# A long convolution with gate and MLP: filter steps three groups apart, and ten pieces of the second batch ahead of the first MLP block

## The chip, the cores and the metric

One NeuronCore of a Trainium2 chip runs the whole program. The metric is the device time of one execution in microseconds. A core has a matrix engine (TensorE, PE in the rows), a vector engine (VectorE, DVE), an activation engine (ScalarE, ACT), a general engine (GpSimd, POOL) and a queue for transfers (SyncE, SP). Each takes its instructions in the order in which the program issues them; between engines there are semaphores.

## The reference

```
h_filt = (relu(pos_emb @ w1) @ w2) * exp(-0.01 * pos)       # (12480, 128)
u = x * v                                                   # (4, 12480, 128)
y = irfft(rfft(u, 2S) * rfft(h_filt, 2S))[:, :S]            # a causal convolution of length S = 12480
a = (x * y).reshape(49920, 128)
h = a @ w_in                                                # (49920, 2048)
g = where(h > 0, h, exp(min(h, 0)) - 1)
out = g @ w_out                                             # (49920, 128)
```

x, v and pos_emb are float32; w_in and w_out are float64, and the kernel converts them itself from pairs of 32-bit words.

## The kernel before, in words

The sequence is seen as 2 x 104 x 60 (w, N1, N2). The convolution is a transform along N1 (a matrix product with a 104 x 104 table, three products of split float32 each, `mm3`), a transform along N2 with a table for every k, a product with the spectrum of the filter, and the two inverses. Between the two directions data goes through DRAM (`a_d`, `h_d`, `f_d`, `b_d`), which turns it.

The program has three parts, each issued in an order written out by hand.

1. **First part**, `stage1` with `first` set, batch 0. 15 groups of input (`g`), each with four pieces (i: two results r, two halves w of the sequence). One piece is one `mm3` into a PSUM tile `aps` and a copy to `a_sb`; `store` sends `a_sb` to `a_d`. Two pieces together are a turn, `q = 2 * g + r`, and every turn also does one of the 30 groups of the filter (class `Filter`): `step` 0 transposes `pos` into `pt` and copies it (ScalarE, `pt_sb`), `step` 1 multiplies by w1 into `rp` and applies Relu (ScalarE, `r_sb`), `step` 2 multiplies by w2 into `hps`, applies the window (VectorE, `h_sb`) and splits into `h_h` (ScalarE) and `h_l` (VectorE). `transform` multiplies by the table into `Hps` (two PSUM banks), which leaves as `hsb` (ScalarE, then VectorE) to `h_d`. In the turns 0 to 15 `weights` converts a piece of w_in or w_out on VectorE (lines 303 to 313) and `split_w` splits the one before (a copy on ScalarE, a subtraction on POOL, line 324). `gate` forms x * v (line 102; POOL from the third group on), `split` its two parts `u_h` (ScalarE) and `u_l` (VectorE, line 111).
2. **Second part**, `stage2` with `first` set: the N2 transforms of batch 0, the filter's spectrum, the product, the inverse, to `b_d`.
3. **MLP**, `Mlp.run`: 120 blocks of 416 tokens with 8 steps each; one step is an `up_proj` (`fps`), `elu`, `split_lo`, `down_proj` (`ops`). `conv_out` does the last inverse of a block (`yps`), `transp` turns it. Beside the steps run side generators: `side[0]` to `side[2]` do `stage1` and `stage2` for the batches 1 to 3, at 1.08 pieces a step, each within the 240 steps of the batch before it.

What sets the order in the first part is the loop of lines 143 to 183 and, ahead of it, lines 121 to 140. In before a turn issues for the next filter group q+1:

```
filt.step(q + 1, 2 * w)       # line 154: step 0 in the first piece, step 2 in the second
...
filt.step(q + 1, 1)           # line 166: step 1, after the first piece
```

Of the kernel before, what the change touches and what calls it, by code (L numbers as in the profile page):

```python
# [14 lines left out]
D = 128  # L15
# [23 lines left out]
def fftconv_gate_elu_mlp_kernel(ctx: ExitStack, tc: tile.TileContext, x, v, pos_emb, w1, w2,  # L39
# [41 lines left out]
    def stage1(st, h, ps_pool, ps_tag, first):  # L81
        Z = 1 if first else 2
        xv = st.enter_context(tc.tile_pool(name=f"xv{h}", bufs=3 if first else 2))
        up = st.enter_context(tc.tile_pool(name=f"up{h}", bufs=2))
        ap = st.enter_context(tc.tile_pool(name=f"ap{h}", bufs=4 if first else 3))
        ld, us, stores = {}, {}, []

        def load(g):
            if g >= NG:
                return  # L90
            xt = xv.tile([N1, 2, G, D], F32, tag="xt", name="xt")
            vt = xv.tile([N1, 2, G, D], F32, tag="vt", name="vt")
            nc.sync.dma_start(out=xt, in_=xq[:, :, h, g * G:(g + 1) * G, :])
            nc.sync.dma_start(out=vt, in_=vq[:, :, h, g * G:(g + 1) * G, :])
            ld[g] = (xt, vt)

        def gate(g):
            if g >= NG:
                return
            xt, vt = ld[g]  # L100
            e = nc.vector if first and g < 2 else nc.gpsimd
            e.tensor_tensor(out=vt, in0=xt, in1=vt, op=ALU.mult)

        def split(g):
            if g >= NG:
                return
            vt = ld.pop(g)[1]
            u_h = up.tile([N1, 2, G, D], F32R, tag="u_h", name="u_h")
            u_l = up.tile([N1, 2, G, D], F32R, tag="u_l", name="u_l")
            copy(u_h, vt)  # L110
            nc.vector.tensor_tensor(out=u_l, in0=vt, in1=u_h, op=ALU.subtract)
            us[g] = (u_h, u_l)

        def store():
            if stores:
                g, r, t = stores.pop()
                nc.sync.dma_start(out=a_d[h][:, r, g * G:(g + 1) * G].rearrange("k n z c -> k (n z c)"),
                                  in_=t.bitcast(F32).rearrange("k n z w d -> k (n z w d)"))

        if first:  # L120
            filt = Filter(st)
            for g in range(4):
                filt.load(g)
                if g < 3:
                    load(g)
                filt.load_w(g)
            gate(0)
            gate(1)
            for q in range(3):
                filt.step(0, q)  # L130
        else:
            load(0)
            load(1)
            for _ in range(4):
                yield
            gate(0)
            gate(1)
            yield
            yield
        split(0)  # L140
        if not first:
            yield
        for g in range(NG):
            if first:
                gate(g + 2)
            u_h, u_l = us.pop(g)
            for i in range(4):
                r, w = divmod(i, 2)
                f = FWD[w][r]
                if w == 0:  # L150
                    a_sb = ap.tile([N1, G, Z, 2, D], F32 if first else F32R, tag="a_sb", name="a_sb")
                if first:
                    q = 2 * g + r
                    filt.step(q + 1, 2 * w)
                ps = ps_pool.tile([N1, 512], F32, tag=ps_tag, name="aps")
                mm3(ps, dft_h[:, f, :], dft_l[:, f, :], u_h[:, w], u_l[:, w])
                src = ps.rearrange("p (n d) -> p n d", n=G)
                if first and w == 0:
                    nc.vector.tensor_copy(out=a_sb[:, :, 0, w], in_=src)
                else:  # L160
                    copy(a_sb[:, :, 0, w], src)
                if not first:
                    nc.vector.tensor_tensor(out=a_sb[:, :, 1, w], in0=src, in1=a_sb[:, :, 0, w], op=ALU.subtract)
                if first:
                    if w == 0:
                        filt.step(q + 1, 1)
                        filt.load(q + 4)
                        filt.load_w(q + 4)
                    else:
                        filt.transform(q)  # L170
                        filt.weights(q)
                        filt.split_w(q - 1)
                if w == 0:
                    store()
                else:
                    stores.append((g, r, a_sb))
                if i == 0:
                    load(g + (3 if first else 2))
                if i == 1:
                    split(g + 1)  # L180
                if i == 2 and not first:
                    gate(g + 2)
                yield
        store()
        if first:
            filt.flush()


    class Filter:
# [2 lines left out]

        def __init__(self, st):
            c1 = st.enter_context(tc.tile_pool(name="c1", bufs=1))
            self.pp = st.enter_context(tc.tile_pool(name="pp", bufs=5))
            self.hp = st.enter_context(tc.tile_pool(name="hp", bufs=1))
            self.wl = st.enter_context(tc.tile_pool(name="wl", bufs=1))
            self.psh = st.enter_context(tc.tile_pool(name="psh", bufs=2, space=PS))
            self.psH = st.enter_context(tc.tile_pool(name="psH", bufs=1, space=PS))
            self.w1 = c1.tile([64, 64], F32, name="w1_sb")  # L200
            self.w2 = c1.tile([64, D], F32, name="w2_sb")
            self.win = c1.tile([N1, 2, N2], F32, name="win_sb")
            nc.scalar.dma_start(out=self.w1, in_=w1)
            nc.scalar.dma_start(out=self.w2, in_=w2)
            nc.scalar.dma_start(out=self.win, in_=window)
            self.pos, self.t, self.hs, self.zs, self.out = {}, {}, {}, {}, []
# [8 lines left out]
        def step(self, g, q):  # L215
# [2 lines left out]
            hp, psh = self.hp, self.psh  # L218
            if q == 0:
                p = self.pos.pop(g)  # L220
                pt = psh.tile([64, 2 * GF, N1], F32, tag="h", name="pt")
                for n in range(2 * GF):
                    nc.tensor.transpose(out=pt[:, n, :], in_=p[:, n // GF, n % GF, :], identity=id_sb[:N1, :N1])
                pt_sb = hp.tile([64, 2 * GF, N1], F32, tag="pt_sb", name="pt_sb")
                copy(pt_sb, pt)
                self.t[g] = pt_sb
            elif q == 1:
                rp = psh.tile([64, 2 * GF, N1], F32, tag="h", name="rp")
                nc.tensor.matmul(out=rp, lhsT=self.w1, rhs=self.t[g], start=True, stop=True)
                r_sb = hp.tile([64, 2 * GF, N1], F32, tag="r_sb", name="r_sb")  # L230
                nc.scalar.activation(out=r_sb, in_=rp, func=ACTF.Relu)
                self.t[g] = r_sb
            elif q == 2:
                r_sb = self.t.pop(g)
                hps = psh.tile([N1, 2, GF, D], F32, tag="h", name="hps")
                for n in range(2 * GF):
                    nc.tensor.matmul(out=hps[:, n // GF, n % GF, :], lhsT=r_sb[:, n, :], rhs=self.w2,
                                     start=True, stop=True)
                h_sb = hp.tile([N1, 2, GF, D], F32, tag="h_sb", name="h_sb")
                nc.vector.tensor_tensor(  # L240
                    out=h_sb, in0=hps,
                    in1=self.win[:, :, g * GF:(g + 1) * GF].rearrange("p w (n o) -> p w n o", o=1).to_broadcast([N1, 2, GF, D]),
                    op=ALU.mult)
                h_h = hp.tile([N1, 2, GF * D], F32R, tag="h_h", name="h_h", bufs=2)
                h_l = hp.tile([N1, 2, GF * D], F32R, tag="h_l", name="h_l", bufs=2)
                hv = h_sb.rearrange("p w n d -> p w (n d)")
                copy(h_h, hv)
                nc.vector.tensor_tensor(out=h_l, in0=hv, in1=h_h, op=ALU.subtract)
                self.hs[g] = (h_h, h_l)

        def transform(self, g):
# [21 lines left out]
        def load_w(self, i):  # L273
# [1 line left out]
            if i >= self.NW:  # L275
                return
            m, c = divmod(i, DFF // WC)
            z = self.wl.tile([128, WC, 2], U32, tag="z", name="z", bufs=5)
            if m == 0:
                src = w_in[:, c * WC:(c + 1) * WC].bitcast(U32)  # L280
                nc.sync.dma_start(out=z.rearrange("p f t -> p (f t)"), in_=src)
# [199 lines left out]
    class Mlp:  # L481
# [12 lines left out]
        def run(self, side, alone):  # L494
# [111 lines left out]
                    b, w, n = blocks[j]  # L606
                    nc.sync.dma_start(out=oq[:, w, b, n * G:(n + 1) * G, :], in_=o)

            for i in range(2):
                load(i)  # L610
            split_b(0)
            split_b(1)
            conv_out(0)
# [54 lines left out]
    with ExitStack() as st:  # L668
# [3 lines left out]
        nc.scalar.dma_start(out=id_sb, in_=ident)  # L672
        copy(dft_h, dft_sb)
        nc.vector.tensor_tensor(out=dft_l, in0=dft_sb, in1=dft_h, op=ALU.subtract)
        psa = st.enter_context(tc.tile_pool(name="psa", bufs=4, space=PS))
        for _ in stage1(st, 0, psa, "a", True):
            pass
    with ExitStack() as st:
# [68 lines left out]
```

## Time and profile before

| | |
|---|---|
| median of 3 runs | 3584.68 us (3576.38 to 3588.11) |
| profiled execution | 3582.95 us, span 3581.2 us |
| busy over the span | PE 3411.3 us (95%), DVE 3156.0 (88%), ACT 2416.0 (67%), POOL 2280.5 (64%) |
| mean granted TensorE clock | 0.975 of 2.4 GHz |
| DMA | 646.30 MB, mean 180 GB/s |

The span runs from the first to the last instruction. Busy shares are means over three parts with different limits, so they are read part by part below. In the rows a time in square brackets is the idle time of the engine just before the instruction, with what ended it; `x4` counts instructions in one row; matmuls overlap, so their own times add up to more than the distance between their starts.

### The profile page before, as it was taken

How to read it: one execution, taken by the hardware profiler on the slowest of the kernel's cores; microseconds unless marked ns; L12 is line 12 of the kernel's file. 1: busy time of each engine (PE TensorE's matmuls, PEld its weight loads, DVE VectorE, ACT ScalarE, POOL GpSimd, SP SyncE). 2: the span in 40 equal slices, each digit the busy share in tenths (PEclk: the TensorE clock that was granted, in tenths of full speed). 3: DMA queues.
4: the chain of work that ended last, by engine and by line, in shares of the span. 5: the costliest groups of instructions: out<-in, count | busy, mean ns of one | idle time of the engine just before them, and what ended most of it. 6: DMA issues, size and time to landing. Idle time of an engine off the chain costs nothing.

```text
span 3581.2 us, 53363 instructions
## 1 busy us (share of the span) xinstructions
PE 3411.3 (95%) x18444; PEld 3153.7 (88%) x18444; DVE 3156.0 (88%) x3941; ACT 2416.0 (67%) x3290; POOL 2280.5 (64%) x1578
## 2 busy tenths in 40 slices
PE   7887888999999999999999999999999999999999
PEld 5666777889899899889999998889999999999998
DVE  5647988999999999999999989989999988888887
ACT  3334546877666677876666677776666677777776
POOL 3406876667777766557677656567676656666565
PEclk7789998999999999999999999999999999999999
DMA  6558876767787744777788746778888842222221
GB/s 185 172 146 245 267 243 175 225 181 210 201 223 215 203 131 143 248 228 216 225 245 230 227 127 175 250 206 227 231 241 225 232 116 58 68 62 58 72 58 27
DMA packets 383995, 646.30 MB, mean 180 GB/s; under 512 B 24678, under 2 KB 170438, under 8 KB 374366
## 3 DMA queue, kind: packets, MB, share of 16 engines
q1 hardware_dynamic: 383305, 642.73, 63.3%
q8 instruction: 147, 2.41, 0.3%
q14 instruction: 122, 1.00, 0.1%
q10 hardware_dynamic: 421, 0.16, 0.0%
HBM read 412.76 MB, written 230.03 MB: 179 GB/s over the span
## 4 chain that ended last, share of the span: by engine, by line
PE 60%; DVE 9%; DMA 7%; issue 4%; ACT 1%; POOL 1%; SPq 1%; POOLq 0%; DVEq 0%; ACTq 0%
PE fps L53 8%; PE fps L55 8%; PE fps L54 8%; PE ops L53 7%; PE ops L54 7%; PE ops L55 7%; DMA al<-a_d 4%; PE bps L445 3%; DVE g_l L576 3%; DVE g L567 2%; PE xps L53 2%; PE xps L55 2%; PE xps L54 2%; DMA vt<-in_v_dram 2%; PE yps L53 1%
## 5 line engine op out<-in xcount | busy, mean ns | idle before, releaser
L570 POOL CAST g_h<-g 128x832 fp32r<-128x832 f32 x960 | 1225.0, 1280 | 979.3 <-DVE g L567 978.7
L560 ACT ACTIVATE n<-fps 128x832 f32<-128x832 f32 x960 | 832.0, 867 | 742.1 <-PE fps L55 723.6
L567 DVE SCALAR_TENSOR_TENSOR g<-n,fps 128x832 f32<-128x832 f32 x960 | 975.2, 1016 | 224.1 <-ACT n L561 219.9
L576 DVE TENSOR_TENSOR g_l<-g,g_h 128x832 fp32r<-128x832 f32 x960 | 1111.2, 1157 | 19.6 <-POOL g_h L570 19.6
L561 ACT ACTIVATE n<-n 128x832 f32<-128x832 f32 x960 | 864.5, 901 | 30.5
L53 PE MATMUL fps<-t_h,wi_h 128*128 128x416 f32 x1920 | 715.6, 373 | 22.4 <-DVE g L567 21.2
L53 PE MATMUL ops<-g_h,wo_h 128*128 128x416 f32 x1920 | 677.0, 353 | 0.5 <-ACT o_sb L58 0.3
L55 PE MATMUL fps<-t_h,wi_l 128*128 128x416 f32 x1920 | 676.0, 352 | 0.0
L54 PE MATMUL fps<-t_l,wi_h 128*128 128x416 f32 x1920 | 675.6, 352 | 0.0
L54 PE MATMUL ops<-g_l,wo_h 128*128 128x416 f32 x1920 | 674.8, 351 | 0.7 <-DVE g_l L576 0.7
L55 PE MATMUL ops<-g_h,wo_l 128*128 128x416 f32 x1920 | 675.1, 352 | 0.0
L426 POOL TENSOR_TENSOR p<-p 120x768 f32<-120x768 f32 x204 | 483.3, 2369 | 76.6 <-DVE p L420 57.7
L53 PEld LDWEIGHTS fps<-t_h,wi_h 128*128 128x128 f32 x1920 | 362.8, 189 | 56.9 <-DVE g L567 36.7
L54 PEld LDWEIGHTS fps<-t_l,wi_h 128*128 128x128 f32 x1920 | 364.6, 190 | 13.4 <-DVE t_l L549 0.3
L53 PEld LDWEIGHTS ops<-g_h,wo_h 128*128 128x128 f32 x1920 | 361.7, 188 | 6.0 <-POOL g_h L570 0.8
L54 PEld LDWEIGHTS ops<-g_l,wo_h 128*128 128x128 f32 x1920 | 362.2, 189 | 4.3 <-DVE g_l L576 1.4
L55 PEld LDWEIGHTS fps<-t_h,wi_l 128*128 128x128 f32 x1920 | 362.1, 189 | 3.1
L55 PEld LDWEIGHTS ops<-g_h,wo_l 128*128 128x128 f32 x1920 | 360.8, 188 | 4.0
L418 DVE TENSOR_TENSOR p<-xps,f 120x512 f32<-120x512 f32 x416 | 283.4, 681 | 10.5 <-ACT a_h L58 4.1
L427 POOL TENSOR_TENSOR p<-p 120x256 f32<-120x256 f32 x204 | 249.4, 1222 | 16.0
L445 PE MATMUL bps<-p,t 120*120 120x256 f32 x832 | 219.5, 386 | 30.5 <-POOL p L427 26.1
L353 DVE TENSOR_TENSOR tl<-t,th 120x360 fp32r<-120x360 f32 x208 | 214.5, 1032 | 25.6 <-ACT th L58 25.4
(95 smaller groups left out, 4966.1 us busy)
## 6 DMA issues: line engine op xcount, KB each, us to landing
a_d<-a_sb SPq DMA_DIRECT2D x90, 832.0 KB
al<-a_d SPq DMA_DIRECT2D x156, 480.0 KB
f<-f_d SPq DMA_DIRECT2D x312, 240.0 KB
b_d<-b_sb SPq DMA_DIRECT2D x156, 480.0 KB
b<-b_d SPq DMA_DIRECT2D x90, 832.0 KB
t<-in_tab_dram SPq DMA_DIRECT2D x208, 281.2 KB
xt<-in_x_dram SPq DMA_DIRECT2D x60, 416.0 KB
vt<-in_v_dram SPq DMA_DIRECT2D x60, 416.0 KB
```

What stands on the lines that cost most here:

```text
L53: nc.tensor.matmul(out=ps, lhsT=hi, rhs=bh, start=start, stop=False)
L54: nc.tensor.matmul(out=ps, lhsT=hi, rhs=bl, start=False, stop=False)
L55: nc.tensor.matmul(out=ps, lhsT=lo, rhs=bh, start=False, stop=stop)
L418: nc.vector.tensor_tensor(out=p[:, :, :2], in0=ps[:, :, 0:1, :].to_broadcast([RI, TG, 2, D]), in1=f[:, :, r], op=ALU.mult)
L426: e.tensor_tensor(out=q, in0=q, in1=p, op=ALU.add)
L427: e.tensor_tensor(out=q[:, :, 1], in0=q[:, :, 1], in1=q[:, :, 2], op=ALU.add)
L445: nc.tensor.matmul(out=ps[:, o], lhsT=t[:, o, 3 * N2:], rhs=y[:, o, :2], start=True, stop=True)
L560: nc.scalar.activation(out=n, in_=ps[:, :, :NT], func=ACTF.Relu, scale=-1.0)
L561: nc.scalar.activation(out=n, in_=n, func=ACTF.Exp, scale=-1.0)
L567: nc.vector.scalar_tensor_tensor(out=g, in0=n, scalar=-1.0, in1=ps[:, :, :NT], op0=ALU.add, op1=ALU.max)
L570: nc.gpsimd.tensor_copy(out=g_h, in_=g)
L576: nc.vector.tensor_tensor(out=g_l, in0=g, in1=g_h, op=ALU.subtract)
```

## The change

```diff
@@ stage1: split
-            nc.vector.tensor_tensor(out=u_l, in0=vt, in1=u_h, op=ALU.subtract)
+            e = nc.gpsimd if first and g else nc.vector
+            e.tensor_tensor(out=u_l, in0=vt, in1=u_h, op=ALU.subtract)
@@ stage1: ahead of the loop
-            for g in range(4):
+            for g in range(5):
                 filt.load(g)
...
             gate(0)
+            for q in range(3):
+                for i in range(3 - q):
+                    filt.step(i, q)
             gate(1)
-            for q in range(3):
-                filt.step(0, q)
         else:
             load(0)
             load(1)
-            for _ in range(4):
+            for _ in range(4 if h > 1 else 0):
                 yield
             gate(0)
             gate(1)
-            yield
-            yield
+            for _ in range(2 if h > 1 else 0):
+                yield
@@ stage1: the loop
-                    filt.step(q + 1, 2 * w)
+                    filt.step(q + 3 - w, w)
...
                     if w == 0:
-                        filt.step(q + 1, 1)
-                        filt.load(q + 4)
-                        filt.load_w(q + 4)
+                        filt.step(q + 1, 2)
+                        filt.load(q + 5)
                     else:
                         filt.transform(q)
-                        filt.weights(q)
-                        filt.split_w(q - 1)
+                        if q % 2 == 0 or q == 1:
+                            c = (q + 1) // 2 + (q > 1)
+                            filt.load_w(c + 5)
+                            filt.weights(c)
+                            filt.split_w(c - 1)
...
         if first:
+            filt.split_w(filt.NW - 1)
             filt.flush()
@@ Filter
-            self.pp = st.enter_context(tc.tile_pool(name="pp", bufs=5))
+            self.pp = st.enter_context(tc.tile_pool(name="pp", bufs=6))
-            self.psh = st.enter_context(tc.tile_pool(name="psh", bufs=2, space=PS))
+            self.psh = st.enter_context(tc.tile_pool(name="psh", bufs=1, space=PS))
-                pt = psh.tile([64, 2 * GF, N1], F32, tag="h", name="pt")
+                pt = psh.tile([64, 2 * GF, N1], F32, tag="t", name="pt")
-                rp = psh.tile([64, 2 * GF, N1], F32, tag="h", name="rp")
+                rp = psh.tile([64, 2 * GF, N1], F32, tag="r", name="rp")
...
-                nc.vector.tensor_tensor(out=h_l, in0=hv, in1=h_h, op=ALU.subtract)
+                nc.gpsimd.tensor_tensor(out=h_l, in0=hv, in1=h_h, op=ALU.subtract)
...
-            z = self.wl.tile([128, WC, 2], U32, tag="z", name="z", bufs=5)
+            z = self.wl.tile([128, WC, 2], U32, tag="z", name="z", bufs=6)
@@ Mlp.run
-            for i in range(2):
-                load(i)
+            for _ in range(1):
+                next(side[0])
+            load(0)
+            load(1)
+            for _ in range(9):
+                next(side[0])
             split_b(0)
             split_b(1)
             conv_out(0)
@@ the first part's PSUM pool
-        psa = st.enter_context(tc.tile_pool(name="psa", bufs=4, space=PS))
+        psa = st.enter_context(tc.tile_pool(name="psa", bufs=3, space=PS))
```

`pt_sb`, `r_sb` and `h_sb` get two buffers each (one before). In PSUM `pt`, `rp` and `hps` have a bank each, where they shared a ring of two, and the transforms' tiles are three, where they were four. A turn now issues `step` 0 of group q+3, `step` 2 of group q+1 and `step` 1 of group q+2. The conversion of the weights stands in turns 0, 1, 2, 4, 6, ... 28, no longer in turns 0 to 15. `u_l` (from the second group on) and `h_l` go from VectorE to POOL. The first ten `next(side[0])` are: the loads, gates and split of the first two groups of batch 1, then nine pieces (27 matmuls).

TensorE in a turn of the first part's loop: the transposes, the first piece's `mm3`, then what stands between it and the second piece's.

```order
-L223 MATMUL pt<-id_sb,pos 64x104 x4
-L53 MATMUL aps<-u_h,dft_h 104x512
-L54 MATMUL aps<-u_l,dft_h 104x512
-L55 MATMUL aps<-u_h,dft_l 104x512
-L229 MATMUL rp<-pt_sb,w_sb 64x416
-L237 MATMUL hps<-w_sb,r_sb 104x128 x4
+L228 MATMUL pt<-id_sb,pos 64x104 x4
+L53 MATMUL aps<-u_h,dft_h 104x512
+L54 MATMUL aps<-u_l,dft_h 104x512
+L55 MATMUL aps<-u_h,dft_l 104x512
+L242 MATMUL hps<-w_sb,r_sb 104x128 x4
+L234 MATMUL rp<-pt_sb,w_sb 64x416
```

`hps` has moved ahead of `rp`, and the two belong to different groups: the `r_sb` that `hps` reads is from the turn before, and so is the `pt_sb` that `rp` reads.

POOL in the loop, two pairs of turns of before:

```order
L324 TENSOR_TENSOR wi_l<-r,wi_h 128x256 x2
L102 TENSOR_TENSOR vt<-xt,vt 104x1024
L324 TENSOR_TENSOR wi_l<-r,wi_h 128x256 x2
L102 TENSOR_TENSOR vt<-xt,vt 104x1024
L324 TENSOR_TENSOR wi_l<-r,wi_h 128x256
```

and the same two pairs with the change:

```order
L112 TENSOR_TENSOR u_l<-vt,u_h 104x1024
L253 TENSOR_TENSOR h_l<-h_sb,h_h 104x512
L102 TENSOR_TENSOR vt<-xt,vt 104x1024
L253 TENSOR_TENSOR h_l<-h_sb,h_h 104x512
L329 TENSOR_TENSOR wi_l<-r,wi_h 128x256
L112 TENSOR_TENSOR u_l<-vt,u_h 104x1024
L253 TENSOR_TENSOR h_l<-h_sb,h_h 104x512
L102 TENSOR_TENSOR vt<-xt,vt 104x1024
L253 TENSOR_TENSOR h_l<-h_sb,h_h 104x512
```

A pair had one gate (L102) and two subtractions of the weights; it has one gate, one subtraction of the weights, one `u_l` and two `h_l`, with `u_l` right behind the weights.

SP from the second part's last stores on, before (`b_d` to `b` and `x` are the blocks of the MLP, `xt` and `vt` batch 1):

```order
L435 DMA b_d_61<-b_sb 120x2x256 x2
L513 DMA b_5089<-b_d_61 104x8x128
L514 DMA x_5088<-in_x_dram 104x512
L513 DMA b_5094<-b_d_61 104x8x128
L514 DMA x_5093<-in_x_dram 104x512
L513 DMA b_5121<-b_d_61 104x8x128
L514 DMA x_5120<-in_x_dram 104x512
L93 DMA xt<-in_x_dram 104x2x512
L94 DMA vt<-in_v_dram 104x2x512
```

and with the change:

```order
L440 DMA b_d_61<-b_sb 120x2x256 x2
L93 DMA xt<-in_x_dram 104x2x512
L94 DMA vt<-in_v_dram 104x2x512
L93 DMA xt<-in_x_dram 104x2x512
L94 DMA vt<-in_v_dram 104x2x512
L518 DMA b_5112<-b_d_61 104x8x128
L519 DMA x_5111<-in_x_dram 104x512
L518 DMA b_5117<-b_d_61 104x8x128
L519 DMA x_5116<-in_x_dram 104x512
L93 DMA xt<-in_x_dram 104x2x512
L94 DMA vt<-in_v_dram 104x2x512
```

Batch 1's first two groups are now asked for ahead of the MLP's first two blocks, and its third ahead of the MLP's third block. On TensorE the nine pieces stand between the second part's last `bps` and the first `yps`.

## Rows read from the trace of the kernel before

**Rows 1.** Stretches: bounds, length, busy PE, PEld, DVE, ACT, POOL; clock, DMA share, GB/s.

```profile
21.00:268.00 247.00, 213.29 (x938) 158.75 (x938) 143.55 (x291) 96.18 (x175) 78.46 (x29) 0.76 0.56 165
320.00:340.00 20.00, 17.99 (x102) 15.41 (x101) 18.46 (x26) 11.14 (x22) 15.84 (x18) 1.00 0.89 279
553.00:567.00 14.00, 11.47 (x58) 9.87 (x57) 12.03 (x11) 10.07 (x13) 10.46 (x7) 1.00 0.41 95
```

**Rows 2.** One line's instructions: line 159, shortest/median/longest ns, first and last start.

```profile
L159 DVE COPY a_sb<-aps x30: 676/679/692, 21.3 to 266.7; 104x512 f32<-104x512 f32 x30
```

**Rows 3.** Order of time on TensorE, first part: start us, length us, instruction.

```profile
228.55 0.91 PE L229 MATMUL rp<-pt_sb,w_sb 64*64 64x416 f32 x2
230.06 1.12 PE L237 MATMUL hps<-w_sb,r_sb 64*104 64x128 f32 x8 [0.60 <-ACT r_sb L231]
...
233.31 0.52 PE L223 MATMUL pt<-id_sb,pos 104*64 104x104 f32 x4
233.60 0.46 PE L53 MATMUL aps<-u_h,dft_h 104*104 104x512 f32 x1
...
235.50 0.91 PE L229 MATMUL rp<-pt_sb,w_sb 64*64 64x416 f32 x2 [0.98 <-ACT pt_sb L58]
...
238.07 0.75 PE L53 MATMUL aps<-u_h,dft_h 104*104 104x512 f32 x1
```

**Rows 4.** Waits, 21 to 268 us: total us, times, longest.

```profile
PE hps L237 <- ACT r_sb L231: 17.4, 29, 0.6
PE rp L229 <- ACT pt_sb L58: 16.2, 18, 1.5
```

**Rows 5.** Stretches of the MLP, lines 163 (first row) and 567 alone: DVE busy (count).

```profile
600.00:650.00 50.00, 10.26 (x16) 1.00 0.77 240
...
600.00:650.00 50.00, 14.15 (x14) 1.00 0.77 240
3050.00:3100.00 50.00, 20.39 (x20) 1.00 0.26 66
```

**Rows 6.** Order of time on TensorE, the MLP's first steps.

```profile
557.16 0.45 PE L53 MATMUL fps<-t_h,wi_h 128*128 128x416 f32 x1 [1.39 <-DVE g L567]
...
571.22 0.48 PE L54 MATMUL aps<-u_l,dft_h 104*104 104x512 f32 x1 [2.62 <-DVE u_l L111]
```

**Rows 7.** Order of time on POOL, first part.

```profile
163.88 3.00 POOL L324 TENSOR_TENSOR wo_l<-r,wo_h 128x256 fp32r<-128x256 f32 x1 [6.97 <-ACT wo_h L58]
...
170.38 0.72 POOL L324 TENSOR_TENSOR wo_l<-r,wo_h 128x256 fp32r<-128x256 f32 x1 [0.95 <-ACT wo_h L58]
171.06 2.34 POOL L102 TENSOR_TENSOR vt<-xt,vt 104x1024 f32<-104x1024 f32 x1
```

**Rows 8.** Order of time on POOL, the MLP's first steps.

```profile
560.62 2.40 POOL L524 TENSOR_TENSOR b<-b,b 104x1024 fp32r<-104x1024 f32 x1
...
564.60 5.48 POOL L102 TENSOR_TENSOR vt<-xt,vt 104x1024 f32<-104x1024 f32 x2
...
582.12 3.43 POOL L102 TENSOR_TENSOR vt<-xt,vt 104x1024 f32<-104x1024 f32 x1
```

**Rows 9.** Groups by line and form, 40 to 268 us: busy us, mean ns.

```profile
L58 ACT ACTIVATE hsb<-Hps 104x512 f32<-104x512 f32 x27 | 16.1, 596 | 37.9 <-PE Hps L55 37.9
...
L58 ACT ACTIVATE wi_h<-r 128x256 fp32r<-128x256 f32 x8 | 3.3, 410 | 0.0
```

**Rows 10.** Order of time on all engines, the start.

```profile
9.89 0.31 SPq L212 DMA_DIRECT2D pos<-in_pos_emb_dram  x1
...
15.37 1.23 DVE L102 TENSOR_TENSOR vt<-xt,vt 104x1024 f32<-104x1024 f32 x1 [4.84 <-DMA vt<-in_v_dram]
```

**Rows 11.** Order of time on all engines, from the second part to the MLP.

```profile
530.42 3.63 SPq L435 DMA_DIRECT2D b_d<-b_sb  x2
...
541.14 1.06 ACT L58 ACTIVATE b<-b 104x1024 fp32r<-104x1024 f32 x1 [7.43 <-DMA b<-b_d]
...
548.60 0.72 PE L53 MATMUL fps<-t_h,wi_h 128*128 128x416 f32 x1 [0.65 <-ACT t_h L58]
```

More of the change, by code (lines that the diff above doesn't have):

```diff
@@ L220, in step @@
                 p = self.pos.pop(g)
-                pt = psh.tile([64, 2 * GF, N1], F32, tag="h", name="pt")
+                pt = psh.tile([64, 2 * GF, N1], F32, tag="t", name="pt")
                 for n in range(2 * GF):
                     nc.tensor.transpose(out=pt[:, n, :], in_=p[:, n // GF, n % GF, :], identity=id_sb[:N1, :N1])
-                pt_sb = hp.tile([64, 2 * GF, N1], F32, tag="pt_sb", name="pt_sb")
+                pt_sb = hp.tile([64, 2 * GF, N1], F32, tag="pt_sb", name="pt_sb", bufs=2)
                 copy(pt_sb, pt)
@@ L227, in step @@
             elif q == 1:
-                rp = psh.tile([64, 2 * GF, N1], F32, tag="h", name="rp")
+                rp = psh.tile([64, 2 * GF, N1], F32, tag="r", name="rp")
                 nc.tensor.matmul(out=rp, lhsT=self.w1, rhs=self.t[g], start=True, stop=True)
-                r_sb = hp.tile([64, 2 * GF, N1], F32, tag="r_sb", name="r_sb")
+                r_sb = hp.tile([64, 2 * GF, N1], F32, tag="r_sb", name="r_sb", bufs=2)
                 nc.scalar.activation(out=r_sb, in_=rp, func=ACTF.Relu)
@@ L238, in step @@
                                      start=True, stop=True)
-                h_sb = hp.tile([N1, 2, GF, D], F32, tag="h_sb", name="h_sb")
+                h_sb = hp.tile([N1, 2, GF, D], F32, tag="h_sb", name="h_sb", bufs=2)
                 nc.vector.tensor_tensor(
```

## The prediction

> **What bounds the kernel now.** I read the stretches of the span first, then the order of time on TensorE inside the first part, then the waits, then the other engines at the two places that the change touches. A *turn* is one filter group with its two transform pieces (lines 147 to 183); there are 30 turns, and two of them, a *pair*, use one group of input.
>
> The first part runs to 268 us. It keeps TensorE busy 213 of 247 us, but at a mean granted clock of 0.76, and moves only 165 GB/s; the second part holds 1.00 and 279 GB/s [rows 1]. So in the first part neither the DMA nor one engine is full. The column copies on line 159 give the pace: 30 of them from 21.3 to 266.7 us, (266.7 - 21.3)/29 = 8.46 us a turn [rows 2]. At full clock one turn shows its make-up: from the `rp` at 228.55 to the `rp` at 235.50 are 6.95 us, in which TensorE waited 0.60 for `r_sb` and 0.98 for `pt_sb` [rows 3]. Its own work is thus 6.95 - 0.60 - 0.98 = 5.37 us. Each wait is a ScalarE copy between two products of the same filter group that stand one behind the other in TensorE's queue; 29 and 18 such waits are in this stretch [rows 4]. After such a turn, at 238.07, a matmul of the same transform takes 0.75 us in place of 0.46 at 233.60 [rows 3]: the waits are paid a second time, through the clock, which goes to 1.2 GHz.
>
> The MLP that follows is bound by TensorE and VectorE together. While side pieces run, 14 MLP steps fit in 50 us and 16 pieces beside them; alone, 20 steps fit [rows 5]. So 50/14 - 50/20 = 1.07 us a step is the price of 16/14 = 1.14 pieces: 0.94 us a piece.
>
> **The change, first part.** The filter's three products of one turn now belong to groups q+3, q+1 and q+2 and have a PSUM bank each, so that every ScalarE copy has most of a turn to finish. Both waits of 0.60 and 0.98 go, and what is late next has to be found.
>
> TensorE: unchanged work, 5.37 us a turn, if the clock stays up. It should: between 553 and 567 us there was a single wait of 1.39 us [rows 6], and the clock of that stretch is 1.00 [rows 1].
>
> POOL takes over `h_l` (each turn) and `u_l` (each pair). The product of 1024 columns takes POOL 2.34 and the subtraction of 256 takes 0.72, which a straight line puts at 1.26 for the 512 columns of `h_l`; bounds 0.72 and 2.34 [rows 7]. `u_l` has the form of POOL's subtraction on line 524, 2.40 [rows 8]. The subtraction of the weights takes 3.00 in 15 of 16 cases, and 0.72 the one time that VectorE converts no weights beside it [rows 7]; in the new order it starts beside a conversion as before, so I take 3.00. In a pair: 3.00 + 2.40 + 2.34 + 2 x 1.26 = 10.3 us, where it had 8.3 at most. VectorE loses `u_l` and two `h_l` a pair and is not waited for.
>
> What is late next is `u_l`. After the last `Hps` of a pair's first turn come ScalarE's `hsb` 0.60, the copy of the weights 0.41 [rows 9], POOL 3.00 for the weights and 2.40 for `u_l`, sum 6.4; I add 0.3 because ScalarE comes to `hsb` late (its `h_h` stands behind VectorE's conversion), 6.7. TensorE meanwhile does a turn, 5.37, and in the next one `pt`, 0.29 from its start to the next, and the first of three matmuls, 0.46 with its tail and some 0.3 without [rows 3], 5.96, and then waits 0.75. A pair is 2 x 5.37 + 0.75 = 11.5 us, POOL's 10.3 fits in it, and a turn is 5.75; I take 5.8. Bounds: 5.37 (no wait) and 6.2 (POOL's `h_l` at 2.34, 12.4 a pair).
>
> DMA: 247 us at 165 GB/s are 40.8 MB, 1.40 MB a turn, which at 5.8 us is 241 GB/s, under the 279 seen [rows 1]. Loads of x and v are asked for about a pair ahead, 11.6 us.
>
> On moving such work to POOL, row and rule part in what they advise. The same product takes VectorE 1.23 [rows 10] and POOL 2.34 [rows 7]. The Trainium skill, "GPSIMD Engine Reference", section "Engine selection", says that elementwise work with two inputs belongs on VectorE, since POOL is about twice as slow. Followed, it would save the 0.75 us of waiting in each of 14 pairs, 11 us; by the rows the sum still falls by the 69 us below, because VectorE's queue is freed of it.
>
> The sum: 29 x (8.46 - 5.8) = 77 us gained. Against it: the first three turns all carry a conversion, one more than the pattern, 3 us (one subtraction at 3.00; bounds 0 and 6). And the start: three groups are transposed first, and the third `pos` was issued at 9.89, behind the second v, which landed at 15.37 [rows 10]. Before, the first group was through its products by then. Now two `rp` and one `hps` come behind, 2 x 0.91 + 1.12 = 2.9 us at full clock, 5.9 at half [rows 3]; I take 5. First part: -77 + 3 + 5 = **-69 us**.
>
> **The change, the ten pieces.** Before, the last store of the second part was issued at 534.05 (530.42 + 3.63), the first block's b was copied at 541.14, and `fps` began at 548.60, 7.5 later [rows 11]. Now four loads of x and v go ahead of b on SP, and 27 matmuls ahead of `conv_out(0)` on TensorE. The ninth computing piece needs the third x and v, whose buffer is free only after the first `u_l`. Of the 7.1 us from the last store to b's copy I give the load 5 (an estimate: the store had to land first). So loads from 534.05 land at 539, then product 2.34, copy about 1, `u_l` 1.23: 543.7. Its load goes behind b; at 5 to 8 us (an estimate from the same 7.1) it lands at 549 to 552, and product, copy, `u_l` and one transform (5.3) put the ninth piece at 554 to 557. Then 7.5 to the first `fps`: 563.5, **15 later** (bounds 10 and 18). In return nine pieces leave the MLP, 9 x 0.94 = 8.5, and so do the two gates that held POOL 5.48 us at 564.60 [rows 8]; TensorE waited 2.62 for the `u_l` behind them [rows 6]. I credit 4, that and some of the other waits of the start-up (bounds 0 and 6). Sum +15 - 8.5 - 4 = +2.5, bounds -4.5 and +9.5. What hides the pieces is the time in which TensorE waited for b; if the loads land late, the delay is bare.
>
> **Sum.** -69 + 2.5 = -66.5. The profiled execution took 3582.95 us (span 3581.2), so 3516.5; the median of the runs shown is 1.7 higher, so **3518 us**.
>
> **Rivals.**
> 1. *The clock stays low.* Speaks for it: three PSUM tiles for the transforms in place of four, one bank per product, and a wait of 0.75 in each pair. Against: the wait of 1.39 us at a clock of 1.00, above [rows 1, 6]. If 0.76 stays, a turn is 5.37/0.76 = 7.1 us, 29 x 1.3 = 38 more: **3556**. The Trainium skill, "TensorE: Matmul & The Clock Gate", section "A second HAM failure mode: psum-queue depth-cycling", describes short idle gaps between groups of matmuls that make the clock swing; by that rule this case would come, while the trace shows it only where two waits stand in one turn. Chance 0.12.
> 2. *POOL never holds TensorE.* The weights' subtraction slips past the conversion (0.72) and a turn is 5.37: 29 x 0.43 = 12 less, **3506**. Chance 0.15.
> 3. *POOL becomes the bound, and slower than before.* Every POOL instruction of a pair is stretched as the weights' subtraction is (by 3.00 - 0.72 = 2.28 for each `h_l`, so 3.5) and as a gate at 582.12 (3.43) [rows 8]: 3.00 + 2 x 3.43 + 2 x 3.5 = 16.9 us, and with 1.2 us for the copies that it waits for a pair is 18.1, a turn 9.0: 29 x 3.2 = 93 more, **3611**. It decides from 16.9 us a pair, the present pace. The Trainium skill, "SBUF — State Buffer", section "Who interferes with whom", has VectorE and POOL lock each other out of a shared port; the trace agrees for the weights' subtraction, 3.00 against 0.72 [rows 7]. Against it: conversions fill only 16 of 30 turns, and a gate without one beside it ran at 2.34 [rows 7]. Chance 0.04.
> 4. *The first part is the DMA's.* If its pattern gives no more than 165 GB/s, the pace stays and only start and pieces count: 3584.7 + 8 + 2.5 = **3595**. Against: the share of 0.56 [rows 1]. Chance 0.04.
>
> **How the numbers follow.** The forecast has 0.65; its own range is 3502 to 3540 (5.4 to 6.2 us a turn, the pieces between -4.5 and +9.5). The range takes in rivals 1 and 2: 3498 to 3558, leaving out the last two and some tails. A measurement of this kernel tells about 0.3%, 11 us, from no change: faster 0.65 + 0.12 + 0.15 = 0.92, the same 0.04 (rival 4), slower 0.04 (rival 3).
>
> **What would show it.** Right: line 161's copies 5.6 to 6.1 us apart, a clock over 0.9 and over 220 GB/s in the first part, the waits of `rp` and `hps` for ScalarE gone, a wait of TensorE for POOL's `u_l` once a pair, the second part beginning about 70 us sooner and lasting the same; from the second part's last store to the first `fps` some 29 us in place of 14.6, and the second batch's transforms done nine pieces sooner. Wrong: a clock near 0.76 without those waits (rival 1), POOL over 0.9 busy (rival 3), DMA share near 0.9 with TensorE idle (rival 4), or an MLP that begins late and gains nothing back.

## The result and the profile after

The changed kernel takes 3550.92 us (median of 5 runs, 3544.8 to 3554.95), against 3580.65 us for the kernel before in the same comparison: a ratio of 0.9916, 95% interval 0.9895 to 0.9937. That is 30 us faster, where 67 us were forecast. The time lies within the stated range of 3498 to 3558 us.

The stretches of the changed kernel (bounds, length, busy PE, PEld, DVE, ACT, POOL; clock, DMA share, GB/s): first the loop of the first part, then a piece of it, then one of the places where the clock falls.

```profile
29.00:228.00 199.00, 186.15 (x931) 132.64 (x929) 105.82 (x247) 89.88 (x172) 147.46 (x71) 0.87 0.66 201
29.00:57.00 28.00, 27.61 (x120) 19.48 (x119) 15.40 (x38) 10.13 (x19) 17.17 (x8) 1.00 0.59 164
...
101.00:114.00 13.00, 13.00 (x44) 9.45 (x44) 5.32 (x14) 5.50 (x10) 9.93 (x6) 0.50 0.66 221
```

The loop's clock is 0.87, where it was 0.76 [rows 1], and it is a mixture: 1.00 in most places, 0.50 in five stretches of 7 to 14 us, which add up to 51 us. In those TensorE is busy without a gap. The first turns are a sixth such stretch that the column does not show. It says 1.00 from 29 us on, but up to 46 us the matmuls have the lengths that they have at 0.50, and a turn, from one `pt` to the next, takes 9.57 us (order of time on TensorE):

```profile
36.91 0.90 PE L228 MATMUL pt<-id_sb,pos 104*64 104x104 f32 x4
37.49 0.73 PE L53 MATMUL aps<-u_h,dft_h 104*104 104x512 f32 x1
...
46.48 0.52 PE L228 MATMUL pt<-id_sb,pos 104*64 104x104 f32 x4
46.78 0.46 PE L53 MATMUL aps<-u_h,dft_h 104*104 104x512 f32 x1
```

The first turns of the other kernels are like this too (up to 30 us in before, up to 38.5 in e9 below), so a clock given here for a loop leaves them out.

The copies that give the pace, by their line (shortest/median/longest ns, first and last start), answering to [rows 2]:

```profile
L161 DVE COPY a_sb<-aps x30: 676/680/692, 29.5 to 228.1; 104x512 f32<-104x512 f32 x30
```

(228.1 - 29.5)/29 = 6.85 us a turn, where 8.46 stood and 5.8 was forecast. The first copy is 8.2 us later than before.

TensorE's waits in the loop (total us, times, longest), answering to [rows 4]:

```profile
PE aps L54 <- POOL u_l L112: 9.0, 10, 2.0
PE hps L242 <- ACT r_sb L236: 2.7, 2, 2.3
```

The waits for ScalarE's copies are gone but for two; a wait for POOL's `u_l` has come. The longer of the two for `r_sb`, 2.29 us at 140.74, has an origin like those of e3 below: an instruction of VectorE's conversion beside POOL's `u_l` took 2.61 us (135.35), and `h_sb`, `h_h` and `r_sb` came late behind it. How a wait for `u_l` goes is to be seen in the order of time on TensorE:

```profile
87.15 0.47 PE L54 MATMUL aps<-u_l,dft_h 104*104 104x512 f32 x1 [0.85 <-POOL u_l L112]
...
98.67 0.48 PE L54 MATMUL aps<-u_l,dft_h 104*104 104x512 f32 x1 [0.85 <-POOL u_l L112]
...
105.27 0.90 PE L228 MATMUL pt<-id_sb,pos 104*64 104x104 f32 x4
107.37 2.03 PE L242 MATMUL hps<-w_sb,r_sb 64*104 64x128 f32 x8
...
114.80 0.52 PE L228 MATMUL pt<-id_sb,pos 104*64 104x104 f32 x4
115.95 1.12 PE L242 MATMUL hps<-w_sb,r_sb 64*104 64x128 f32 x8
...
120.01 0.52 PE L228 MATMUL pt<-id_sb,pos 104*64 104x104 f32 x4
```

Two waits of 0.85 us, one pair apart. After the first the clock stays up; after the second it falls, and the turn from 105.27 to 114.80 takes 9.5 us, with no wait in it. The turn from 114.80 to 120.01, at full clock again, takes 5.2.

POOL, in the same pair, does what the prediction had it do (start, length):

```profile
93.08 3.02 POOL L329 TENSOR_TENSOR wi_l<-r,wi_h 128x256 fp32r<-128x256 f32 x1 [1.04 <-ACT wi_h L58]
96.06 2.56 POOL L112 TENSOR_TENSOR u_l<-vt,u_h 104x1024 fp32r<-104x1024 f32 x1
98.58 1.27 POOL L253 TENSOR_TENSOR h_l<-h_sb,h_h 104x512 fp32r<-104x512 f32 x1
99.81 2.36 POOL L102 TENSOR_TENSOR vt<-xt,vt 104x1024 f32<-104x1024 f32 x1
```

At the other place, from the second part to the MLP, the order of time on all engines, answering to [rows 11]:

```profile
495.18 0.32 SPq L440 DMA_DIRECT2D b_d<-b_sb  x1
...
502.29 2.34 POOL L102 TENSOR_TENSOR vt<-xt,vt 104x1024 f32<-104x1024 f32 x1 [12.01 <-DMA vt<-in_v_dram]
505.77 0.76 PE L53 MATMUL aps<-u_h,dft_h 104*104 104x512 f32 x1 [11.30 <-ACT u_h L58]
507.00 0.32 SPq L94 DMA_DIRECT2D vt<-in_v_dram  x1
515.21 2.38 POOL L102 TENSOR_TENSOR vt<-xt,vt 104x1024 f32<-104x1024 f32 x1 [6.00 <-DMA vt<-in_v_dram]
520.59 0.75 PE L53 MATMUL aps<-u_h,dft_h 104*104 104x512 f32 x1 [1.70 <-DVE a_sb L165]
529.89 0.71 PE L53 MATMUL fps<-t_h,wi_h 128*128 128x416 f32 x1 [0.61 <-ACT t_h L58]
```

From the end of the last store's issue (495.5) to the first `fps` are 34.4 us, 19.8 more than before. The MLP from its first to its last `fps` (line 53, first and last start), before and after:

```profile
L53 PE MATMUL fps<-t_h,wi_h x1920: 346/353/716, 548.6 to 3568.5; 128*128 128x416 f32 x192
```

```profile
L53 PE MATMUL fps<-t_h,wi_h x1920: 346/353/713, 529.9 to 3538.6; 128*128 128x416 f32 x192
```

3019.9 and 3008.7 us: 11.2 regained. So the profiled execution, 29.9 us shorter, splits into +8.2 (start), -46.8 (29 turns), about 0 (from the loop to the second part's end) and +8.6 (pieces: 19.8 - 11.2). Forecast: +5, -74 (77 less the 3 for the early conversions), 0 and +2.5. **The loop holds 27 of the 37 us that are missing**; it is the main question.

### The profile page after: what moved, and what is told of

Read it like the earlier page. It is cut to its first block, busy times and chain, and to the rows that moved or that the text cites. A ratio compares the mean times of both kernels' runs of the same rounds, so it can differ in the third digit from the quotient of the medians.

```text
span 3551.3 us, 53404 instructions
## 1 busy us (share of the span) xinstructions
PE 3394.7 (96%) x18444; PEld 3131.3 (88%) x18444; DVE 3114.3 (88%) x3897; ACT 2410.1 (68%) x3290; POOL 2355.2 (66%) x1622
## 4 chain that ended last, share of the span: by engine, by line
PE 59%; DVE 10%; DMA 7%; issue 4%; ACT 1%; POOL 1%; SPq 1%; POOLq 0%; DVEq 0%; ACTq 0%
PE fps L53 8%; PE fps L55 8%; PE fps L54 8%; PE ops L53 7%; PE ops L54 7%; PE ops L55 7%; DMA al<-a_d 3%; DVE g_l L581 3%; PE bps L450 3%; DVE g L572 2%; DMA vt<-in_v_dram 2%; PE xps L53 2%; PE xps L55 2%; PE xps L54 2%; PE yps L53 1%
## 5 line engine op out<-in xcount | busy, mean ns | idle before, releaser
L581 DVE TENSOR_TENSOR g_l<-g,g_h 128x832 fp32r<-128x832 f32 x960 | 1111.4, 1158 | 18.3 <-POOL g_h L575 18.3
```

Of the source, the lines that this page charges most:

```text
L581: nc.vector.tensor_tensor(out=g_l, in0=g, in1=g_h, op=ALU.subtract)
```

## The experiments

The theories on the loop. **A**: TensorE's waits bring the clock down, whichever engine they are for; without them it stays up and a turn takes what TensorE needs. **B**: it falls whatever the waits (three PSUM tiles for the transforms, one bank for each product). All twelve kernels, each beside runs of the kernel before on its own chip:

| kernel | median us | ratio to before, 95% |
|---|---|---|
| the change | 3550.92 | 0.9895 to 0.9937 |
| e1: first part alone | 3539.77 | 0.9863 to 0.9908 |
| e2: ten pieces alone | 3589.36 | 1.0009 to 1.0050 |
| e3: `u_l` ahead of the weights | 3562.67 | 0.9937 to 0.9967 |
| e4: `u_l` on VectorE | 3557.44 | 0.9914 to 0.9959 |
| e5: e3, and `rp` ahead of `hps` | 3550.43 | 0.9902 to 0.9945 |
| e6: five pieces that compute, not nine | 3540.76 | 0.9874 to 0.9920 |
| e7: `pos` ahead at the start | 3544.52 | 0.9874 to 0.9919 |
| e8: `rp` ahead of `hps` alone | 3547.14 | 0.9880 to 0.9928 |
| e9: e5, conversion in the other turn | 3518.60 | 0.9813 to 0.9864 |
| e10: e9, e7, no pieces | 3504.76 | 0.9763 to 0.9811 |
| e11: e9, e7, five pieces | 3506.36 | 0.9769 to 0.9817 |
| e12: e9, e7, all ten | 3519.08 | 0.9801 to 0.9850 |

### The two halves apart: e1 and e2

e1 takes the ten `next(side[0])` out of the change, with the yields of `stage1` as before; e2 puts these same lines into the kernel before.

> The changed kernel with the ten pieces back in the MLP (the second batch's transforms wait four and two steps again), the first part as changed. Theory: the first part alone gives 38.5 us of the gain and the ten pieces cost 8.6 of it, so this kernel should be 8 to 9 us faster than the change (about 3542), its first fps some 19.8 us sooner after the second part's last store (14.6 us), and its first part should show the same clock of about 0.87. Rival: the pieces cost nothing net (within 3 us), the 8.6 is a difference of the two profiled executions.

> The kernel before with the ten pieces in front of the first MLP block and nothing else. Theory: 5 to 10 us slower than before (3586 to 3591): first fps 20 us later after the last store, the MLP regains 11. Rival (my forecast): +2.5, between -4.5 and +9.5.

By the medians e1 is 11 us faster than the change (their intervals overlap a little), and e2, clear of the noise, 6.7 slower than the kernel before. From the last store to the first `fps` e1 has 14.3 us, e2 35.1. The pieces cost (e12 below says so a third time); the first part gives the whole gain. e2's trace shows one more thing: its first part, the same instructions as before, was over 8.4 us sooner (last store to `h_d` at 261.53 in place of 269.93). A single profiled first part is that uncertain, as long as its clock swings: the change's own loop, unedited in e1 and e6, took 194.9 and 192.6 us there, in place of 198.6.

### One wait away, another comes: e3 and e4

```diff
+                if first and i == 1:
+                    split(g + 1)
                 if first:
                     if w == 0:
...
-                if i == 1:
+                if i == 1 and not first:
                     split(g + 1)
```

> The changed kernel with the next group's u_h and u_l issued in front of the transform and the conversion of the weights in the same turn, so that POOL makes u_l before the subtraction of the weights and not behind it. Theory A (the clock falls because TensorE waits for u_l): the wait for u_l goes, the clock of the stretch 29 to 230 rises from 0.87 to above 0.95, a turn goes from 6.85 to 5.4 to 5.8, 25 to 35 us faster than the change: about 3520. Theory B (the clock falls whatever the wait, by the three PSUM tiles or other short gaps): the wait goes, clock and time stay within 5 us of the change.

e4 instead gives `u_l` back to VectorE (`e = nc.vector` in `split`).

> The changed kernel with u_l of the first part back on VectorE in its old place behind the conversion. Theory A: u_l then waits for VectorE's conversion of the weights (about 3 us) and stands behind it, but no longer behind POOL's 3.0; if TensorE waits less for it, the clock rises and the kernel is 10 to 25 us faster than the change; if VectorE comes to it later than POOL did, the waits stay and the time is the same or slower by up to 15. Theory B: clock and time as the change within 5 us.

e3 is 12 us slower than the change by the medians, which neither theory had. Its waits (up to 230 us), its loop, and VectorE and POOL at one conversion:

```profile
PE hps L244 <- ACT r_sb L238: 16.1, 10, 2.6
```

```profile
29.00:241.00 212.00, 193.02 (x930) 138.85 (x929) 112.10 (x247) 90.18 (x172) 114.51 (x71) 0.81 0.62 188
```

```profile
96.29 2.37 POOL L112 TENSOR_TENSOR u_l<-vt,u_h 104x1024 fp32r<-104x1024 f32 x1 [1.82 <-ACT u_h L58]
98.33 1.17 DVE L303 TENSOR_SCALAR k<-z 128x256 uint32<-128x256 uint32 x1
98.62 0.72 POOL L331 TENSOR_TENSOR wi_l<-r,wi_h 128x256 fp32r<-128x256 f32 x1
99.42 0.28 DVE L303 TENSOR_SCALAR f<-z 128x256 uint32<-128x256 uint32 x1
```

The wait for `u_l` is gone, and the weights' subtraction takes 0.72 in place of 3.02. Now it is the conversion that is late: its first instruction takes 1.17 in place of 0.28 and ends 0.2 us behind POOL's work. Behind the conversion on VectorE stands `h_sb`, ScalarE's `h_h` waits for that, and behind `h_h` stands `r_sb`, for which TensorE now waits. The wait of TensorE behind this conversion is 0.89 us; before the longest ones (2.59 us at 117.28) `hsb`, which VectorE does ahead of the conversion, also stood behind `u_h` on ScalarE. More waits, lower clock, longer time: with A, but its number for this order was wrong. e4 ends up the same way (`r_sb` 18.3 us in 13 waits, clock 0.86).

### Two and three waits away: e8, e5 and e9

e8 issues `step` 1 of group q+2 ahead of `step` 2 of group q+1; e5 is e3 with that:

```diff
-                    filt.step(q + 3 - w, w)
+                    if w == 0:
+                        filt.step(q + 3, 0)
...
                     if w == 0:
+                        filt.step(q + 2, 1)
                         filt.step(q + 1, 2)
```

> The changed kernel with rp and r_sb ahead of hps and h_h, u_l left behind the weights' subtraction. Theory A: the ten waits for u_l stay, so the clock stays at 0.85 to 0.90 and the time within 6 us of the change. Rival (the two long waits for r_sb are what brings the clock down): clock above 0.93 and 15 to 25 us faster.

> The run before it (u_h and u_l ahead of the weights) took away the wait for u_l and brought a new one: TensorE waited 10 times, up to 2.6 us, for r_sb, which stands on ScalarE behind an h_h that waits for VectorE's conversion; its clock was 0.80. Here the product rp and its r_sb are issued ahead of hps, h_sb and h_h as well, so that r_sb waits for nothing of VectorE. Theory A (waits of 0.8 to 2.6 us, whichever engine TensorE waits for, bring the clock down): both waits go, clock of 29 to 230 above 0.95, a turn 5.3 to 5.6 us, about 35 us faster than the change: 3510 to 3525. Theory B (the clock falls whatever the waits: three PSUM tiles, short gaps): no waits, yet clock 0.80 to 0.88 and 3545 to 3565. Theory C (a third wait takes their place, the POOL and VectorE conversion locking each other out): a new row in TensorE's waits of over 5 us in total, clock below 0.92.

e8 keeps its ten waits for `u_l` and lies within 6 us of the change; its clock, 0.93 up to the loop's end at 218 us, is a little above what A had, and its profiled loop, 188.6 us, is 10 us shorter than the change's. In e5 theory C came true: a third wait. Its waits:

```profile
PE hps L246 <- DVE h_sb L249: 9.1, 8, 2.0
PE Hps L53 <- DVE hsb L271: 2.7, 7, 0.4
```

The clock to the loop's end is 0.87 and the time the change's. The `hps` of the next turn needs its one bank back, and the `h_sb` that frees it stands behind the conversion. e9 therefore also moves the conversion to the other turn of the pair, behind `h_sb`:

```diff
                         filt.step(q + 1, 2)
                         filt.load(q + 5)
+                        if q % 2 or q == 0:
+                            c = (q + 1) // 2
+                            filt.load_w(c + 5)
+                            filt.weights(c)
                     else:
                         filt.transform(q)
-                        if q % 2 == 0 or q == 1:
...
+                        if q % 2:
+                            filt.split_w((q - 1) // 2)
```

> The last three orders each traded one wait of TensorE for another: u_l behind the weights' subtraction, r_sb behind h_h, and, with both moved, hps for its single PSUM bank, since VectorE's h_sb stands behind the conversion of the weights (8 waits, up to 2.0 us, clock 0.86). Here, beside those two moves, the conversion itself goes to the other turn of the pair, behind h_sb and not ahead of it, where POOL has only one h_l to do. Theory A (any wait of about 1 to 2.6 us brings the clock down, and without them it stays up): no wait of TensorE over 5 us in total, clock of 29 to 230 above 0.95, copies on line 161's place 5.2 to 5.6 us apart on average, 30 to 40 us faster than the change: 3512 to 3522. Theory B (the clock falls whatever the waits): no such waits and clock 0.80 to 0.90, 3540 to 3555. Theory C: a further wait.

The stretch of e9's loop, its waits in it, and its copies:

```profile
31.00:187.00 156.00, 155.41 (x927) 112.95 (x927) 108.80 (x242) 91.02 (x170) 129.49 (x70) 1.00 0.77 251
```

```profile
PE Hps L53 <- DVE hsb L272: 0.5, 1, 0.5
```

```profile
L162 DVE COPY a_sb<-aps x30: 673/680/691, 31.1 to 185.8; 104x512 f32<-104x512 f32 x30
```

One wait of 0.5 us, which stands behind the last copy (185.91), a clock of 1.00 from 38.5 us on, (185.8 - 31.1)/29 = 5.33 us a turn, and 32 us less than the change. PSUM is as in the change, with its three tiles. Against e5, TensorE's instructions and their order are the same; only the conversion has moved, on the other engines, and with it 11.8 us of waits have gone. So **B is refuted, and A holds**: without waits the clock stays up. (That every wait brings it down is not shown; see below.) The profiled execution is the fastest of e9's five. The slower ones, up to 3528 us, have a mean clock of 0.986 to 0.988 in place of 0.989; where theirs falls no trace shows.

The loop is 43.9 us shorter than the change's. Of that 11.7 is waits (the 9.0 and 2.7 above). The change has 51 us of falls (199 x 0.13/0.5 = 52 by the mean clock), and the half clock of its first turns lasts some 9 us longer than in e9. A turn takes 9.5 us at half clock and 5.2 at full, so 4.3 of 9.5 us are lost, 27 of these 60 us (an estimate from the turns shown above). Some 5 us of the difference are not assigned.

### The start and the number of pieces: e7, e6, e10 to e12

e7 issues the second and third `pos` right behind the first v; e6 puts `range(5)` where the change has `range(9)`.

> The changed kernel with the second and third pos issued behind the first v and ahead of the first weights and the second x and v. Theory (the start is 8.2 us later because the third transposition, at 17.05, waits for its pos behind the second v): third pt at 11 to 13, first a_sb copy at 24 to 26 in place of 29.5, 3 to 5 us faster than the change. Rival (the start's copies on ScalarE and the second v set it): first a_sb copy at 28 or later, no gain.

> The changed kernel with six of the ten pieces (the loads and five that compute) in front of the first MLP block; the third group of x and v is then not waited for there. Theory (the last four pieces, which wait for the third v's load, cost more in the delay of the first fps than the MLP regains for them): first fps about 10 us after the kernel before's distance from the last store (24 to 26 us in place of 34.4), 3 to 7 us faster than the change. Rival (each piece costs as much before the MLP as it saves in it): same time within 2 us.

e7's first copy comes at 25.25 in place of 29.52, as forecast; its time, 6 us less, is not told apart from the change's (the intervals overlap). e6 is 10 us faster than the change by medians (the intervals overlap), though its profiled execution, 10 us over the median, has 28.5 us from store to `fps`, not 24 to 26, and regains under 1 us in the MLP.

> The run before it, with the second and third pos ahead of the second x and v and the ten pieces back in the MLP. By the runs so far the start gives 4 us and the pieces 8 to 11: 12 to 15 us faster than the run before it, 3498 to 3510 if theory A holds there. Rival: the gains do not add up, since a first part that ends sooner waits for its DMA: within 6 us of the run before it.

> As the run before it, with six pieces (five that compute) in front of the first MLP block in place of none. With ten in place of none the kernel was 11 us slower, with six in place of ten 10 us faster; so six and none should come out within 4 us of each other. Rival: none is better by over 5 us.

> The order of the last two runs, with all ten pieces in front of the first MLP block: with them it gives none, six and ten on the same first part, whose clock stays up. Theory (ten pieces delay the first fps by 20 us and the MLP regains 9 to 14): 7 to 11 us slower than with none, 3512 to 3516; since six came out 2 us from none, the last four are then what costs. Rival (number of pieces is indifferent): within 4 us of 3505.

All ten against none cost 14 us here (7 to 11 were expected), 11 in e1 against the change and 6.7 in e2 against before. Six against none cost 1.6 and 1.0 us (e11 against e10, e6 against e1), so by the medians it is the last four that cost; they need the third group of x and v. In the profiled executions six delay the first `fps` by 12.4 us against none (27.1 in e11, 14.7 in e10) and the MLP gives back 3 of it, so there e11's first part makes up for it, and where six pieces get their time back stays open. e12 comes out where e9 does although its first copy is at 24.5 and not at 31.1: the start's gain of 4 to 6 us is seen in rows, but not in this time.

e10 is one more witness for A. Behind its first turns its loop has one fall, with the second of two waits (order of time on TensorE; then the stretches between the two and behind the second):

```profile
84.52 0.36 PE L53 MATMUL Hps<-h_h,dft_h 104*104 104x256 f32 x1 [1.58 <-DVE hsb L277]
...
97.16 0.54 PE L53 MATMUL Hps<-h_h,dft_h 104*104 104x256 f32 x1 [1.94 <-DVE hsb L277]
```

```profile
85.00:93.00 8.00, 8.00 (x51) 5.69 (x50) 5.38 (x13) 5.76 (x11) 5.60 (x4) 1.00 0.80 256
98.00:109.00 11.00, 11.00 (x40) 8.17 (x40) 4.99 (x14) 4.76 (x8) 5.54 (x3) 0.50 0.64 187
```

e11, with the same first part, had no such wait and no fall up to 181 us, behind its first turns, and sent its last store to `h_d` at 183.6 us in place of 192.9.

**A version better than both**: e10 and e11, at 3505 us 2.1% faster than the kernel before and 46 us faster than the change. The two are not told apart.

## Why the prediction was right or wrong

**The late operand: right.** "Then waits 0.75" in each pair: 0.85 was the common length, 11.7 us of waits in the loop where 0.75 in 14 pairs is 10.5. A pair at full clock takes 11.5 us as forecast (POOL's `u_l` starts at 84.53 and 96.06), TensorE's own work is 5.2 to 5.3 us a turn (5.37 forecast), and POOL's durations are 3.02, 2.56, 2.36 and 1.27 against 3.00, 2.40, 2.34 and 1.26. The waits of `rp` for ScalarE went, and those of `hps` but for two.

**The clock: the step that failed.** "TensorE: unchanged work, 5.37 us a turn, if the clock stays up. It should", because a "single wait of 1.39 us" stood in a stretch with a clock of 1.00 [rows 6, 1]. That was read too narrowly. The wait was not single, and the stretch ended 5 us ahead of a fall: behind the wait of 2.62 us at 571.22 [rows 6] the clock went to half. From the order of time on TensorE and the stretches, before:

```profile
564.88 0.45 PE L53 MATMUL fps<-t_h,wi_h 128*128 128x416 f32 x1 [0.87 <-DVE g L567]
```

```profile
572.00:576.00 4.00, 4.00 (x14) 3.66 (x13) 4.00 (x5) 2.32 (x3) 2.06 (x2) 0.57 0.40 107
```

So the trace of before already had a fall in the MLP, where rival 1 says that it shows one only in turns with two waits. The change's loop has twelve waits, and five came with a fall to 0.50: all three of 1.5 us and more, and two of the six of 0.84 to 0.86 us. The same length did both: 0.85 us at 87.15 without a fall, at 98.67 with one. So the loop's 74 us (77 less 3) came out as 46.8; the falls lost some 23 (51 x 4.3/9.5, an estimate), and the half clock of the first turns, which the forecast had not priced either, some 8 (17 x 4.3/9.5); that is 31 where 27 are missing, and against it a turn at full clock took 5.2 us in place of 5.37. Rival 1 had the mechanism, priced for a clock of 0.76 all through; it came half way, at 0.87. That the time of 3551 is near rival 1's 3556 is in part luck: the loop lost 27 of the 38 us that it priced, and the start and the pieces, 9 us worse than forecast, made up the rest. What it cited is borne out in part: the Trainium skill, "TensorE: Matmul & The Clock Gate", section "A second HAM failure mode: psum-queue depth-cycling", lays a swinging clock to short idle gaps between groups of matmuls, and the trace agrees; the cycling through PSUM banks that it names is not the cause here, since e9 keeps the banks of the change and has, behind its first turns, no gaps and no falls up to the loop's end.

**The engine for `u_l`.** The forecast put 11 us against the change because VectorE is the faster of the two for such work (1.23 against 2.34 us [rows 10, 7]). e4 gave `u_l` back to it: 6.5 us slower than the change by the medians, not told apart, and in any case not 11 faster, because `r_sb` then came late behind VectorE's queue. Which queue an operation stands in counted for more than how fast its engine is: e9 leaves both subtractions on POOL and has no wait for them.

**The start: mis-sized.** 5 forecast, 8.2 measured. The cause of half of it was the named one, the third `pos` behind the second v: e7 takes 4.3 back. The other 3.9 no run takes apart.

**The ten pieces: mis-sized.** The delay was 19.8, forecast 15 (bounds 10 and 18); the gain in the MLP 11.2, forecast 12.5. The first load took 6.8 us from the store (502.3 - 495.5; 5 given), the third v 8.2 (507.0 to 515.2; 5 to 8 given), and the pieces ran at a clock of 0.50, behind an idle time of TensorE of 11.30 us: each matmul at 0.63 and more, which the 15 had not taken in. Net +8.6 in place of +2.5, inside the bounds of -4.5 and +9.5, though the delay itself lay outside of its own.

**Rivals 2, 3 and 4** did not come: TensorE was held, POOL was busy 147 of 199 us, and the DMA moved 201 GB/s at a share of 0.66 (e9: 251 at 0.77). The forecast's own range, 3502 to 3540, comes out as 3499 to 3537 by its terms; nothing hangs on the 3 us.

## What to carry to other kernels

Where a change leaves a short wait of TensorE in every round of a loop, price the loop at full clock and at what the clock gives after such waits, not at the wait alone: here 12 us of waits cost some 23 more through the clock. Take the waits away to the last one before judging an order: three orders that each traded one wait for another were not told apart from the change or were slower (e3, e5, e8), and the fourth, without any, came to the time that was forecast (3519 us). A stretch that is to show that a wait costs no clock must be read on behind its end. The wait to look for next is found one queue further back: what stands in front of the late operand on its engine, and which buffer waits for that.

## What the runs showed of the hardware

- After one wait of 0.85 us TensorE ran at 0.50 for some 14 us, busy without a gap, before the clock came back; after a wait of the same length one pair earlier it stayed at 1.00. e10 had 1.58 us at 84.52 without a fall and 1.94 us at 97.16 with one. In the change both waits of 0.85 and 0.86 us with a fall were the second of two, one pair apart; whether that is what tells the cases apart no run shows.
- VectorE and POOL hold each other up in both directions. In the change POOL's subtraction of the weights, begun 0.25 us ahead of a conversion, took 3.02 us and the conversion's first seven instructions 0.28 each; in e3, where POOL was in the midst of `u_l` when the conversion came, POOL kept its 2.37 and 0.72 and the conversion's first instruction took 1.17. In the change one instruction of a conversion beside `u_l` took 2.61 in place of 0.41 (line 317, at 135.35 and 95.08). The Trainium skill, "SBUF — State Buffer", section "Who interferes with whom", calls the port that the two share an exclusive lock; these rows agree.
